# Attention maxima four heads at a time, in seven PSUM banks shared with the scores

## The chip, the cores and the metric

The kernel runs on one core of one Trainium2 chip. A core has TensorE (matmuls; PE in the profile, with its weight loads shown apart as PEld), VectorE (DVE), ScalarE (ACT), GpSimd (POOL) and SyncE (SP), which issues the transfers here. Matmul results go to PSUM, which this kernel uses as eight banks of 128 partitions by 512 float32 values; ScalarE and VectorE read them there. The metric is the device time of one execution in microseconds (us); lower is better.

## The reference

Two attentions over the same 2048 tokens (448 features, 16 heads of 28) are mixed by a gate per token:

```python
g = sigmoid((x * gate_w).sum(-1, keepdims=True))
# A: linear attention, feature maps phi = [softmax(q w_phi), softmax(-q w_phi)]
num = einsum("bhqf,bhfd->bhqd", phi_q, kv);  den = phi_q . z + 1e-6;  a = (num / den) @ wo_A
# B: softmax attention
scores = einsum("bhqd,bhkd->bhqk", q, k) * Dh ** -0.5
p = softmax(scores, axis=-1)
b = einsum("bhqk,bhkd->bhqd", p, v) @ wo_B
out = g * a + (1 - g) * b
```

The change touches only B. Its softmax subtracts, for each query and head, the largest score over all 2048 keys; these are the maxima of this document.

## The kernel before, in words

The front stage (to about 340 us) projects q, k and v, does attention A and computes the maxima of the first few batches. A batch `gq` is one group of four heads with one block of 512 queries; there are 16 batches. Then comes the attention stage of B: 256 steps `s`, sixteen to a batch, one for each block of 128 keys.

The order of the work is written out by hand on TensorE, VectorE, ScalarE and GpSimd: each engine runs its instructions in the order of the program, and a semaphore holds an instruction whose input or target isn't ready. Weight loads stand in TensorE's own order, so a load that waits holds everything behind it. A step issues, in this order:

- `scores(s, 0)` and `scores(s, 1)` (matmuls L831, exponentials L833): four matmuls, keys by queries, one per head, 128x512 each. The negated maxima are a row of the operands, so that the scores come out already shifted. Two heads fill a pair of banks, and one exponential on ScalarE reads both (128x1024).
- `values(s - 1)` (L934): the four heads' exponentials of the step before, times v, added up over sixteen steps in one bank, `pv`.
- `finish` after the sixteenth: VectorE and ScalarE copy `pv` out (L373); the normalization follows over the next ten steps, with a small reciprocal on VectorE, two products on GpSimd and a cast on ScalarE.
- `mx_visit()` (matmuls L306, reduction L314): a visit to the maxima of a later batch. Three scores of 128 queries by 512 keys go to a tile of three banks (four heads lie at four groups of 32 rows, so that the matmuls of different heads go side by side), and one reduction on VectorE takes the three largest values (128x1536 to 128x3). There are 720 such scores in this stage. After the last of a batch, `mx_reduce` appends three small VectorE instructions (L232, L236, L238), which run behind the next visit's reduction.

In the last group of heads, twelve steps also project an output tile (`project`, L108 and L948), followed by a second visit.

PSUM's eight banks: two pairs for scores (`ps2`), three for maxima (`psm`), one for `pv`. When all maxima are done, `spare_open` turns the three into a third pair and a bank for projections, and `tail_open` into three banks for the last output tiles.

Of the kernel before, what the change touches and what calls it, by code (L numbers as in the profile page):

```python
# [8 lines left out]
F32 = mybir.dt.float32  # L9
F32R = mybir.dt.float32r  # L10
U32 = mybir.dt.uint32
AF = mybir.ActivationFunctionType
ALU = mybir.AluOpType
AX = mybir.AxisListType
PSUM = bass.MemoryType.PSUM
DRAM = bass.MemoryType.DRAM

P = 128
S = 2048
D = 448  # L20
H = 16
DH = 28
GW = 112
NG = 4
NT = S // P
NQ = S // 512
SCALE = DH ** -0.5
# [12 lines left out]
def gated_mix_kernel(ctx, tc, xT, wqkB, wvB, wvA, wkAT, wqAT, phi, woA, woB,  # L40
# [7 lines left out]
    nc = tc.nc  # L48
# [35 lines left out]
    sel_s = const.tile([P, 4], F32, name="sel_s")  # L84
# [70 lines left out]
    mxs = {"u": 0, "f": 0, "fin": []}  # L155
# [3 lines left out]
    part = mxp.tile([P, NU * 4], F32, name="part", bufs=1)  # L159
# [24 lines left out]
    def mx_query(gq):  # L184
        g, qb = divmod(gq, NQ)
        mxs[("qc", gq)] = mx_rows(mx_tile("qc", f"qc{gq}", 3), range(4), q_d[g], range(4), qb * 512)
# [100 lines left out]
    def mx_visit():  # L287

        fins = mxs["fin"][:]
        mxs["fin"].clear()  # L290
        f = mxs["f"]
        todo = flats[f:f + 3]
        todo = [x for i, x in enumerate(todo) if x[4] == todo[0][4] + i]
        if not todo:
            for fn in fins:
                fn()
            return
        mxs["f"] = f + len(todo)
        pm = psm.tile([P, 3, 512], F32, tag="mx", name=f"pm{f}", bufs=1)
        for i, (gq, kb, qt, j, col) in enumerate(todo):  # L300
            g, qb = divmod(gq, NQ)
            if kb == 1 and qt in (0, QM) and j == 0 and gq + 1 < NG * NQ:
                if ("qc", gq + 1) not in mxs:
                    mx_query(gq + 1)
            js = slice(32 * j, 32 * j + DH)
            nc.tensor.matmul(pm[:, i, :], mxs[("qc", gq)][js, qt * P:(qt + 1) * P],  # L306
                             mxs[("kc", g, kb)][js, :], start=True, stop=True,
                             tile_position=(32 * j, 0))
            if j == 3 and qt == 3 and qb == NQ - 1 and g + 1 < NG:
                mx_load(g + 1, kb)  # L310
            if kb == 3 and qt == 3 and j == 3:
                mx_reduce(gq)
        n, col = len(todo), todo[0][4]
        nc.vector.tensor_reduce(part[:, col:col + n], pm[:, :n], AX.X, ALU.max)  # L314
        for fn in fins:
            fn()

# [501 lines left out]
    def scores(s, i):  # L819

        gq, kt = divmod(s, NT)
        g, qb = divmod(gq, NQ)
        if s:
            p = late_p.tile([P, 2, 512], F32, tag="p", name=f"p{s}_{i}", bufs=6)
            st = ps_p(f"st{s}_{i}", s == NS - 1)
        else:
            p = at.tile([P, 2, 512], F32, name=f"p{s}_{i}")
            st = ps_mx(f"st{s}_{i}", i)
        for jl in range(2):
            j = 2 * i + jl  # L830
            nc.tensor.matmul(st[:, jl, :], kst_of[(g, kt // 4)][:, j, (kt % 4) * P:(kt % 4 + 1) * P],  # L831
                             qst_of[gq][:, j, :], start=True, stop=True)
        nc.scalar.activation(p, st, AF.Exp, scale=SCALE)  # L833
        pts.setdefault(s, []).append(p)

    qst = [stack("qst0", False)]
    kst = [stack(f"kst{i}", True) for i in range(5)]
# [24 lines left out]
    ps_s_.close()  # L862
    fr_s.close()
    ps2 = ctx.enter_context(tc.tile_pool(name="ps2", bufs=1, space=PSUM, reuse_waits="tile"))
    psm_s, spare_s = ExitStack(), ExitStack()
    psm = psm_s.enter_context(tc.tile_pool(name="psm", bufs=1, space=PSUM, reuse_waits="tile"))

    spare = []
    turns = {"n": 0}

    def spare_open():
        psm_s.close()
        spare.append(spare_s.enter_context(
            tc.tile_pool(name="psx", bufs=1, space=PSUM, reuse_waits="tile")))

    def ps_p(nm, last=False):
        if spare and spare[0] is not None and not last:
            turns["n"] += 1
            if turns["n"] % 3 == 0:
                return spare[0].tile([P, 2, 512], F32, tag="p", name=nm, bufs=1)  # L880
        return ps2.tile([P, 2, 512], F32, tag="p", name=nm, bufs=2)

    late_p = ctx.enter_context(tc.tile_pool(name="late", bufs=1, reuse_waits="tile"))
    woB_s = late_p.tile([P, 2, 4, D], F32R, name="woB_s")
# [42 lines left out]
    def values(s):  # L927
        gq, kt = divmod(s, NT)
        g, qb = divmod(gq, NQ)
        if kt == 0:  # L930
            pv_of[gq] = ps2.tile([P, 512], F32, tag="pv", name=f"pv{gq}", bufs=1)
        pv, pt = pv_of[gq], pts.pop(s)
        for j in range(4):
            nc.tensor.matmul(pv[32 * j:32 * j + 32, :], vb[kt // 8][:, kt % 8, 4 * g + j, :],  # L934
                             pt[j // 2][:, j % 2, :],
                             start=kt == 0, stop=kt == NT - 1, tile_position=(0, 32 * j),
                             skip_group_check=True)

    def project(qb, oT, tl):

        t = qb * 4 + tl
        acc = acc_of[qb][:, tl, :]
        if spare:
            po = spare[0].tile([P, 512], F32, tag="po", name=f"pob{t}", bufs=1)
        else:
            po = ps_p(f"pob{t}")[:, 0, :]
        run(po[:, :D], first_passes(qb, tl) + out_passes(oT, tl * P, woB_s, NG - 1))
        nc.vector.scalar_tensor_tensor(acc, po[:, :D], gate1[:, t:t + 1], acc,  # L948
                                       op0=ALU.mult, op1=ALU.add)
        nc.sync.dma_start(out[0, t * P:(t + 1) * P, :], acc)  # L950
# [7 lines left out]
    tail = {"todo": []}  # L958

    def tail_open():  # L960
        spare_s.close()
        spare[0] = None
        pst = ctx.enter_context(tc.tile_pool(name="pst", bufs=1, space=PSUM, reuse_waits="tile"))
        tail["po"] = [pst.tile([P, 512], F32, name=f"poL{i}")[:, :D] for i in range(3)]
        for tl in range(4):
            tail["todo"] += [(tl, i == 0, x) for i, x in enumerate(first_passes(NQ - 1, tl))]

    def tail_fill(n):
        for _ in range(min(n, len(tail["todo"]))):
            tl, first, (l, r) = tail["todo"].pop(0)  # L970
            if tl == len(tail["po"]):
                tail["po"].append(ps_p("poL3")[:, 0, :D])
            nc.tensor.matmul(tail["po"][tl], l, r, start=first, stop=False,
                             skip_group_check=True)

# [34 lines left out]
    def finish_last(gq):  # L1010

        oU = late_p.tile([P, 512], F32, tag="oU", name="oUlast", bufs=2)
        nc.vector.tensor_copy(oU, pv_of[gq])
        tail_fill(4)
        pd = ps_p("pd")
        for tl in range(4):
            nc.tensor.matmul(pd[:, 0, 4 * tl:4 * tl + 4], oU[:, tl * P:(tl + 1) * P], sel_s,
                             start=True, stop=True)
        rc = late_p.tile([P, 16], F32, tag="den", name="rc", bufs=2)
        nc.vector.reciprocal(rc, pd[:, 0, :16])  # L1020
        oT = late_p.tile([P, 2, 512], F32R, tag="oT", name="oTlast", bufs=2)
        rw = late_p.tile([P, 16, 32], F32, tag="rs", name="rw", bufs=2)
        nc.vector.tensor_copy(rw, rc.unsqueeze(2).to_broadcast([P, 16, 32]))
        tail_fill(4)
        pr = pd[:, 1, :]
        for tl in range(4):
            nc.tensor.matmul(pr[:, tl * P:(tl + 1) * P],
                             rw[:, 4 * tl:4 * tl + 4, :].rearrange("p j d -> p (j d)"), ident,
                             start=True, stop=True)
        tail_fill(12)  # L1030
        for c in (0, 256):
            nc.vector.tensor_mul(oU[:, c:c + 256], oU[:, c:c + 256], pr[:, c:c + 256])
            nc.scalar.copy(oT[:, 0, c:c + 256], oU[:, c:c + 256])
        for c in (0, 256):
            nc.vector.tensor_sub(oT[:, 1, c:c + 256], oU[:, c:c + 256], f32(oT[:, 0, c:c + 256]))
        for tl in range(4):
            while tail["todo"] and tail["todo"][0][0] <= tl:
                tail_fill(1)
            po, t = tail["po"][tl], (NQ - 1) * 4 + tl
            acc = acc_of[NQ - 1][:, tl, :]  # L1040
            for i, (l, r) in enumerate(out_passes(oT, tl * P, woB_s, NG - 1)):
                nc.tensor.matmul(po, l, r, start=False, stop=i == 2, skip_group_check=True)
            nc.vector.scalar_tensor_tensor(acc, po, gate1[:, t:t + 1], acc,
                                           op0=ALU.mult, op1=ALU.add)
            nc.sync.dma_start(out[0, t * P:(t + 1) * P, :], acc)
# [9 lines left out]
    for s in range(NS + 16):  # L1055
# [29 lines left out]
            mx_fin()  # L1085
        if s in mids:
            mids.pop(s)()
            mx_visit()
        if mxs["f"] == len(flats) and not spare:
            spare_open()  # L1090
        if NG * NQ - 1 in nm_of and NG * NQ - 1 in qst_of:
# [71 lines left out]
```

## Time and profile before

| what | value |
|---|---|
| median of three runs | 1054.67 us (1054.39 to 1055.61) |
| the profiled execution | 1055.21 us |
| its span, first to last instruction | 1053.2 us |
| granted TensorE clock | 0.999 |
| busy: TensorE, ScalarE, VectorE, GpSimd | 99%, 69%, 67%, 22% of the span |
| exponentials (ScalarE, L833) | 512 of 1.02 us |
| reductions of maxima (VectorE, L314) | 241 |

A group's row gives line, engine, operation, names of tiles (out<-in), shapes and count, then busy time in us, the mean duration in ns, and the idle time of the engine just before with what ended it. A row in order of time gives start and length in us. The span is what the instructions cover; the time of an execution has about 2 us more around it. Matmuls are pipelined and their ends are modelled, so starts are the better measure on TensorE.

### The profile page before, as it was taken

The page shows a single profiled execution, that of the slowest core. Times are in us where ns is not written, and L with a number is a line of the kernel's source. Part 1 is how long each engine was busy: PE and PEld are TensorE (multiplying, and loading weights), DVE is VectorE, ACT ScalarE, POOL GpSimd, SP SyncE. Part 2 cuts the span into 40 slices and gives each one's busy share as a digit, 9 for nine tenths or more (in the row PEclk, how much of TensorE's full clock was granted, in tenths as well). Part 3 has the DMA queues.
Part 4 walks back from the last instruction along what each step waited for, and adds up shares of the span by engine and source line. Part 5 has one row for each costly group of instructions (what it writes and reads, how often), then busy time and mean ns, then how long its engine had stood idle before and what let it go on. Part 6 is the DMA issues. An engine that isn't in the chain of part 4 may idle for free.

```text
span 1053.2 us, 16588 instructions
## 1 busy us (share of the span) xinstructions
PE 1042.9 (99%) x6344; PEld 568.8 (54%) x6344; DVE 705.6 (67%) x872; ACT 726.7 (69%) x878; POOL 227.3 (22%) x189
## 2 busy tenths in 40 slices
PE   8999999999999999999999999999999999999998
PEld 7777777778777634334433433443343343454545
DVE  5476776897856567767776777677677777777302
ACT  5355555577855777887777777777777777747572
POOL 1234454678635500120000000000000000000000
PEclk9999999999999999999999999999999999999999
DMA  8873110122233832233522324422233344132311
GB/s 292 292 234 101 42 38 30 41 66 88 86 111 93 186 64 53 62 77 78 121 63 68 80 54 145 116 65 71 64 69 78 83 108 104 46 112 65 96 63 53
DMA packets 64183, 99.03 MB, mean 94 GB/s; under 512 B 18008, under 2 KB 24776, under 8 KB 64104
## 3 DMA queue, kind: packets, MB, share of 16 engines
q1 hardware_dynamic: 64104, 97.97, 34.0%
q8 instruction: 50, 0.82, 0.4%
q14 instruction: 29, 0.24, 0.1%
HBM read 69.77 MB, written 27.78 MB: 93 GB/s over the span
## 4 chain that ended last, share of the span: by engine, by line
PE 93%; DVE 5%; ACT 1%; POOL 1%; DMA 0%; issue 0%; DVEq 0%; ACTq 0%; POOLq 0%
PE st L831 27%; PE pv L934 24%; PE pm L306 10%; PE pqk L108 5%; PE poa L108 4%; PE pk L126 4%; PE pva L126 3%; PE pob L108 3%; PE pmb L267 3%; PE pvb L126 2%; PE pvb L108 2%; PE pq L108 1%; PE pn L507 1%; PE pft L495 1%; PE pqk L609 1%; DVE rl L272 1%
## 5 line engine op out<-in xcount | busy, mean ns | idle before, releaser
L833 ACT ACTIVATE p<-st 128x1024 f32<-128x1024 f32 x512 | 496.7, 1022 | 165.0 <-PE st L831 163.5
L314 DVE TENSOR_REDUCE part<-pm 128x3 f32<-128x1536 f32 (+1 forms) x241 | 421.9, 1751 | 168.5 <-PE pm L306 168.3
L831 PE MATMUL st<-qst,kst 128*128 128x512 f32 x1024 | 306.6, 421 | 0.0
L934 PE MATMUL pv<-p,vb 128*32 128x512 f32 x2048 | 272.7, 605 | 0.0
L831 PEld LDWEIGHTS st<-qst,kst 128*128 128x128 f32 x1024 | 172.5, 188 | 92.5 <-issue 67.4
L306 PEld LDWEIGHTS pm<-kc,qc 28*128 28x128 f32 x720 | 45.2, 181 | 199.4 <-DVE part L314 175.7
L272 DVE CUSTOM_DVE_ANT_0 rl<-pmb,rl 128x512 f32<-128x512 f32 x152 | 98.2, 684 | 54.8 <-ACT rl L270 54.7
L394 POOL TENSOR_TENSOR oUb<-oUb,rsb 128x512 f32<-128x512 f32 x15 | 19.2, 1282 | 518.4 <-DMA rsb<-rdb 313.7
L306 PE MATMUL pm<-kc,qc 28*128 28x512 f32 x720 | 121.2, 495 | 0.4 <-DVE part L314 0.4
L270 ACT ACTIVATE rl<-pmd 128x1024 f32<-128x1024 f32 x76 | 78.1, 1028 | 38.6 <-PE pmd L267 30.1
L934 PEld LDWEIGHTS pv<-p,vb 128*32 128x32 f32 x2048 | 40.3, 108 | 93.6 <-issue 92.8
L108 PE MATMUL pqk<-XH,wB 128*128 128x512 f32 x192 | 59.6, 397 | 1.7 <-DVE ev L547 1.7
L108 PE MATMUL poa<-woA_s,oTa 128*128 128x448 f32 x192 | 43.4, 375 | 0.0
L546 ACT CAST ev<-pqk 128x512 fp32r<-128x512 f32 x28 | 15.9, 588 | 36.5 <-PE pqk L108 32.1
L108 PEld LDWEIGHTS pqk<-XH,wB 128*128 128x128 f32 x192 | 35.3, 188 | 10.5 <-DVE ev L547 2.1
L126 PE MATMUL pk<-wkA_s,XH 128*128 128x448 f32 x128 | 39.4, 381 | 0.0
L267 PE MATMUL pmd<-kp,qp 28*128 28x512 f32 x152 | 37.9, 494 | 1.0 <-DVE part L272 1.0
L108 PEld LDWEIGHTS poa<-woA_s,oTa 128*128 128x128 f32 x192 | 34.9, 188 | 6.3 <-issue 3.3
L267 PE MATMUL pmb<-kp,qp 28*128 28x512 f32 x152 | 38.0, 495 | 0.0
L126 PE MATMUL pva<-wvA_s,XH 128*128 128x450 f32 x128 | 37.8, 371 | 0.0
L108 PE MATMUL pq<-wqA_s,XH 128*128 128x448 f32 x128 | 37.3, 374 | 0.2 <-ACT oUa L370 0.2
L948 DVE SCALAR_TENSOR_TENSOR acc<-pob,gate,acc 128x448 f32<-128x448 f32 x12 | 8.2, 684 | 41.6 <-PE pob L108 41.6
(150 smaller groups left out, 1072.7 us busy)
## 6 DMA issues: line engine op xcount, KB each, us to landing
qkd<-ev SPq DMA_DIRECT2D x28, 512.0 KB
qst<-qkd SPq DMA_DIRECT2D x64, 224.0 KB
kst<-qkd SPq DMA_DIRECT2D x64, 224.0 KB
od<-oTb SPq DMA_DIRECT2D x48, 112.0 KB
rsa<-rda SPq DMA_DIRECT2D x8, 512.0 KB
rsb<-rdb SPq DMA_DIRECT2D x15, 256.0 KB
gad<-ga SPq DMA_DIRECT2D x16, 224.0 KB
acc<-gad SPq DMA_DIRECT2D x4, 896.0 KB
```

The source lines that it names most:

```text
L108: nc.tensor.matmul(dst, l, r, start=i == 0, stop=i == len(todo) - 1)
L126: nc.tensor.matmul(dst[:, :n], l, r, start=i == 0, stop=i == len(todo) - 1, skip_group_check=True)
L267: nc.tensor.matmul((pb if j < 2 else pd)[:, j % 2, :], qc[js, qt * P:(qt + 1) * P], kc[js, :], start=True, stop=True, tile_position=(32 * ...
L270: nc.scalar.activation(rl, pd, AF.Relu)
L272: nc.vector.tensor_tensor_reduce(rl[:, i, :], pb[:, i, :], rl[:, i, :], 1.0, LOWEST, ALU.add, ALU.max, part[:, col + i:col + i + 1])
L306: nc.tensor.matmul(pm[:, i, :], mxs[("qc", gq)][js, qt * P:(qt + 1) * P], mxs[("kc", g, kb)][js, :], start=True, stop=True, tile_position= ...
L314: nc.vector.tensor_reduce(part[:, col:col + n], pm[:, :n], AX.X, ALU.max)
L394: (nc.gpsimd if n == 1 else nc.vector).tensor_mul(oU, oU, rs)
L546: nc.scalar.copy(e[:, 0, :], pq)
L831: nc.tensor.matmul(st[:, jl, :], kst_of[(g, kt // 4)][:, j, (kt % 4) * P:(kt % 4 + 1) * P], qst_of[gq][:, j, :], start=True, stop=True)
L833: nc.scalar.activation(p, st, AF.Exp, scale=SCALE)
L934: nc.tensor.matmul(pv[32 * j:32 * j + 32, :], vb[kt // 8][:, kt % 8, 4 * g + j, :], pt[j // 2][:, j % 2, :], start=kt == 0, stop=kt == NT ...
```

## The change

One pool of seven banks (`free`, tags g0 to g6) serves scores and maxima. Each score takes one bank off the front of the list, gets an exponential of its own (128x512; 1024 of them and no longer 512) and its own tile of results. A visit takes four banks for the four heads of one query block against one key block, four matmuls and four reductions of one bank each, so that there are 180 visits. The visit's first bank goes back on the list at once; the other three wait in `held` and are returned, interleaved with the step's four score banks, behind the second `scores` of the next step. Returning a bank to the list is a matter of the program's text: whoever takes it waits, on the chip, for the instruction that last reads it. The second visit behind a projection is gone. After the last visit the held banks go back and one bank is set aside for projections; the end of the kernel takes its banks from the same list.

```diff
-        todo = flats[f:f + 3]
-        todo = [x for i, x in enumerate(todo) if x[4] == todo[0][4] + i]
...
+        todo = flats[f:f + 4]
         mxs["f"] = f + len(todo)
-        pm = psm.tile([P, 3, 512], F32, tag="mx", name=f"pm{f}", bufs=1)
...
+            pm = mx_banks(f)
+            for j in range(4):
+                js = slice(32 * j, 32 * j + DH)
+                nc.tensor.matmul(pm[j], mxs[("qc", gq)][js, qt * P:(qt + 1) * P],
+                                 mxs[("kc", g, kb)][js, :], start=True, stop=True,
+                                 tile_position=(32 * j, 0))
+            for j in range(4):
+                nc.vector.tensor_reduce(part[:, col + j:col + j + 1], pm[j], AX.X, ALU.max)
...
-        n, col = len(todo), todo[0][4]
-        nc.vector.tensor_reduce(part[:, col:col + n], pm[:, :n], AX.X, ALU.max)
         for fn in fins:
             fn()
@@ scores(s, i) @@
-        if s:
-            p = late_p.tile([P, 2, 512], F32, tag="p", name=f"p{s}_{i}", bufs=6)
-            st = ps_p(f"st{s}_{i}", s == NS - 1)
...
-        nc.scalar.activation(p, st, AF.Exp, scale=SCALE)
-        pts.setdefault(s, []).append(p)
+        sts = []
+        for j in (2 * i, 2 * i + 1):
+            used.append(free.pop(0))
+            sts.append(bank(used[-1], f"st{s}_{j}"))
+            score(j, sts[-1])
+        for st in sts:
+            p = late_p.tile([P, 512], F32, tag="p", name=f"p{s}_{len(pts.get(s, []))}", bufs=12)
+            nc.scalar.activation(p, st, AF.Exp, scale=SCALE)
+            pts.setdefault(s, []).append(p)
+        if i == 1:
+            a, m = used[:], held[:]
+            free.extend([a[0], m[0], a[1], m[1], a[2], a[3], m[2]] if m else a)
+            used.clear()
+            held.clear()
@@ pools @@
+    free, used, held = list(range(7)), [], []
+    def bank(i, nm):
+        return ps2.tile([P, 512], F32, tag=f"g{i}", name=nm, bufs=1)
+
+    def mx_banks(f):
+        b = [free.pop(0) for _ in range(4)]
+        free.append(b[0])
+        held.extend(b[1:])
+        return [bank(i, f"pm{f}_{j}") for j, i in enumerate(b)]
 
     def spare_open():
+        free.extend(held)
+        held.clear()
+        spare.append(free.pop())
@@ project @@
-        if spare:
-            po = spare[0].tile([P, 512], F32, tag="po", name=f"pob{t}", bufs=1)
-        else:
-            po = ps_p(f"pob{t}")[:, 0, :]
+        po = bank(spare[0], f"pob{t}")
@@ the loop over steps @@
         if s in mids:
             mids.pop(s)()
-            mx_visit()
```

More of the change, by code (lines that the diff above doesn't have):

```diff
@@ L291, in mx_visit @@
         f = mxs["f"]
-        todo = flats[f:f + 3]
-        todo = [x for i, x in enumerate(todo) if x[4] == todo[0][4] + i]
[L294 to L297, printed above, removed]
+        todo = flats[f:f + 4]
         mxs["f"] = f + len(todo)
-        pm = psm.tile([P, 3, 512], F32, tag="mx", name=f"pm{f}", bufs=1)
-        for i, (gq, kb, qt, j, col) in enumerate(todo):
+        if todo:
+            gq, kb, qt, _, col = todo[0]
             g, qb = divmod(gq, NQ)
[L302 to L309, printed above, removed]
+            if kb == 1 and qt in (0, QM) and gq + 1 < NG * NQ and ("qc", gq + 1) not in mxs:
+                mx_query(gq + 1)
+            pm = mx_banks(f)
[6 more added lines that the diff above has]
+                nc.vector.tensor_reduce(part[:, col + j:col + j + 1], pm[j], AX.X, ALU.max)
+            if qt == 3 and qb == NQ - 1 and g + 1 < NG:
                 mx_load(g + 1, kb)
-            if kb == 3 and qt == 3 and j == 3:
+            if qt == 3 and kb == 3:
                 mx_reduce(gq)
-        n, col = len(todo), todo[0][4]
-        nc.vector.tensor_reduce(part[:, col:col + n], pm[:, :n], AX.X, ALU.max)
         for fn in fins:
@@ L822, in scores, with score @@
         g, qb = divmod(gq, NQ)
-        if s:
-            p = late_p.tile([P, 2, 512], F32, tag="p", name=f"p{s}_{i}", bufs=6)
-            st = ps_p(f"st{s}_{i}", s == NS - 1)
-        else:
+        def score(j, st):
+            nc.tensor.matmul(st, kst_of[(g, kt // 4)][:, j, (kt % 4) * P:(kt % 4 + 1) * P],
+                             qst_of[gq][:, j, :], start=True, stop=True)
+        if s == 0:
             p = at.tile([P, 2, 512], F32, name=f"p{s}_{i}")
             st = ps_mx(f"st{s}_{i}", i)
[L829 to L833, printed above, removed]
-        pts.setdefault(s, []).append(p)
+            for jl in range(2):
+                score(2 * i + jl, st[:, jl, :])
+            nc.scalar.activation(p, st, AF.Exp, scale=SCALE)
+            pts.setdefault(s, []).extend([p[:, 0, :], p[:, 1, :]])
+            return
+        sts = []
[5 more added lines that the diff above has]
+            p = late_p.tile([P, 512], F32, tag="p", name=f"p{s}_{len(pts.get(s, []))}", bufs=12)
+            nc.scalar.activation(p, st, AF.Exp, scale=SCALE)
+            pts.setdefault(s, []).append(p)
[4 more added lines that the diff above has]
+            held.clear()
     qst = [stack("qst0", False)]
@@ L864, in gated_mix_kernel @@
     ps2 = ctx.enter_context(tc.tile_pool(name="ps2", bufs=1, space=PSUM, reuse_waits="tile"))
-    psm_s, spare_s = ExitStack(), ExitStack()
-    psm = psm_s.enter_context(tc.tile_pool(name="psm", bufs=1, space=PSUM, reuse_waits="tile"))
+    free, used, held = list(range(7)), [], []
     spare = []
-    turns = {"n": 0}
-    def spare_open():
[L872 to L881, printed above, removed]
+    def bank(i, nm):
[5 more added lines that the diff above has]
+        return [bank(i, f"pm{f}_{j}") for j, i in enumerate(b)]
+    def spare_open():
+        free.extend(held)
+        held.clear()
+        spare.append(free.pop())
     late_p = ctx.enter_context(tc.tile_pool(name="late", bufs=1, reuse_waits="tile"))
@@ L934, in values @@
             nc.tensor.matmul(pv[32 * j:32 * j + 32, :], vb[kt // 8][:, kt % 8, 4 * g + j, :],
-                             pt[j // 2][:, j % 2, :],
+                             pt[j],
                              start=kt == 0, stop=kt == NT - 1, tile_position=(0, 32 * j),
@@ L942, in project @@
         acc = acc_of[qb][:, tl, :]
-        if spare:
-            po = spare[0].tile([P, 512], F32, tag="po", name=f"pob{t}", bufs=1)
-        else:
-            po = ps_p(f"pob{t}")[:, 0, :]
+        po = bank(spare[0], f"pob{t}")
         run(po[:, :D], first_passes(qb, tl) + out_passes(oT, tl * P, woB_s, NG - 1))
@@ L960, in tail_open @@
     def tail_open():
[L961 to L964, printed above, removed]
+        tail["po"] = [bank(i, f"poL{n}")[:, :D]
+                      for n, i in enumerate([spare[0], free.pop(0), free.pop(0)])]
         for tl in range(4):
@@ L971, in tail_fill @@
             if tl == len(tail["po"]):
-                tail["po"].append(ps_p("poL3")[:, 0, :D])
+                tail["po"].append(bank(free.pop(0), "poL3")[:, :D])
             nc.tensor.matmul(tail["po"][tl], l, r, start=first, stop=False,
@@ L1014, in finish_last @@
         tail_fill(4)
-        pd = ps_p("pd")
+        pd = bank(free.pop(0), "pd")
         for tl in range(4):
-            nc.tensor.matmul(pd[:, 0, 4 * tl:4 * tl + 4], oU[:, tl * P:(tl + 1) * P], sel_s,
+            nc.tensor.matmul(pd[:, 4 * tl:4 * tl + 4], oU[:, tl * P:(tl + 1) * P], sel_s,
                              start=True, stop=True)
         rc = late_p.tile([P, 16], F32, tag="den", name="rc", bufs=2)
-        nc.vector.reciprocal(rc, pd[:, 0, :16])
+        nc.vector.reciprocal(rc, pd[:, :16])
         oT = late_p.tile([P, 2, 512], F32R, tag="oT", name="oTlast", bufs=2)
@@ L1024, in finish_last @@
         tail_fill(4)
-        pr = pd[:, 1, :]
+        pr = bank(free.pop(0), "pr")
         for tl in range(4):
```

## The prediction

> **What bounds the kernel now.** I read the page first (busy shares, chain, groups), then the order of time inside one step of the attention stage, then the few rows that price a short instruction or a late one.
>
> ```profile
> span 1053.2 us, 16588 instructions
> ...
> PE 1042.9 (99%) x6344; PEld 568.8 (54%) x6344; DVE 705.6 (67%) x872; ACT 726.7 (69%) x878; POOL 227.3 (22%) x189
> ...
> PE 93%; DVE 5%; ACT 1%; POOL 1%; DMA 0%; issue 0%; DVEq 0%; ACTq 0%; POOLq 0%
> PE st L831 27%; PE pv L934 24%; PE pm L306 10%; PE pqk L108 5%; PE poa L108 4%; PE pk L126 4%; PE pva L126 3%; PE pob L108 3%; PE pmb L267 3%; PE pvb L126 2%; PE pvb L108 2%; PE pq L108 1%; PE pn L507 1%; PE pft L495 1%; PE pqk L609 1%; DVE rl L272 1%
> ...
> L314 DVE TENSOR_REDUCE part<-pm 128x3 f32<-128x1536 f32 (+1 forms) x241 | 421.9, 1751 | 168.5 <-PE pm L306 168.3
> ```
>
> TensorE is the path: the chain that ended last is 93% TensorE, and 27 + 24 + 10% of it are scores (L831), values (L934) and maxima (L306). VectorE and ScalarE work two thirds of the span. The reduction of the maxima runs 241 times. In order of time, one step (start and length in us):
>
> ```profile
> 602.35 1.20 PE L831 MATMUL st<-qst,kst 128*128 128x512 f32 x4
> 603.48 1.06 PE L934 MATMUL pv<-p,vb 128*32 128x512 f32 x8
> 604.48 0.50 PE L306 MATMUL pm<-kc,qc 28*128 28x512 f32 x3
> 604.91 1.21 PE L831 MATMUL st<-qst,kst 128*128 128x512 f32 x4
> 605.03 1.76 DVE L314 TENSOR_REDUCE part<-pm 128x3 f32<-128x1536 f32 x1 [0.81 <-PE pm L306]
> 605.73 0.40 PE L831 MATMUL st<-qst,kst 128*128 128x512 f32 x1
> 605.75 1.94 ACT L833 ACTIVATE p<-st 128x1024 f32<-128x1024 f32 x2 [0.63 <-PE st L831]
> ```
>
> A step lasts 2.56 us (602.35 to 604.91). TensorE passes from scores to values after 1.13 (602.35 to 603.48), from values to maxima after 1.00, from maxima to the next scores after 0.43 (604.48 to 604.91). VectorE waits 0.81 per step and ScalarE 0.63: neither holds TensorE up. The steps after the last maxima:
>
> ```profile
> 998.03 1.19 PE L831 MATMUL st<-qst,kst 128*128 128x512 f32 x4
> 999.15 1.06 PE L934 MATMUL pv<-p,vb 128*32 128x512 f32 x8
> 1000.15 1.19 PE L831 MATMUL st<-qst,kst 128*128 128x512 f32 x4
> ```
>
> 2.12 us. A visit of maxima costs TensorE 0.435 us, between the 0.43 above and this difference of 0.44.
>
> **The change, part by part.** (a) *Fewer visits.* 720 heads of maxima in threes took 241 visits (the cut between two batches costs one); in fours they take 180. A visit's price does not grow with the fourth head if four row tiles go side by side as three do. The front stage has four such matmuls in a unit:
>
> ```profile
> 271.79 0.50 PE L267 MATMUL pmd<-kp,qp 28*128 28x512 f32 x2
> 272.22 0.84 PEld L495 LDWEIGHTS pft<-ident,featq 128*112 128x112 f32 x8 [0.25 <-issue]
> ```
>
> Next work again 0.43 after their start. So 61 x 0.435 = 26.5 us less on TensorE. The visits then end at step 180 and not near step 236.
>
> (b) *Projections.* Eight of the twelve mid-step projections had a second visit behind them and shared the pairs of banks:
>
> ```profile
> 917.48 0.76 PEld L831 LDWEIGHTS st<-qst,kst 128*128 128x128 f32 x4 [0.24 <-issue]
> 922.90 0.76 PEld L831 LDWEIGHTS st<-qst,kst 128*128 128x128 f32 x4 [0.25 <-issue]
> ```
>
> and, behind the last visit,
>
> ```profile
> 1019.25 0.86 PEld L831 LDWEIGHTS st<-qst,kst 128*128 128x128 f32 x4
> 1023.62 0.86 PEld L831 LDWEIGHTS st<-qst,kst 128*128 128x128 f32 x4
> ```
>
> 5.42 less two visits (0.87) is 4.55, against 4.37 without visits: 8 x 0.15 = 1.2 us less.
>
> (c) *The hand-out of banks.* Before, maxima had three banks of their own and the two pairs of scores had two each. Followed by hand, the new list settles at once: scores 1 and 2 of a step take the banks of scores 3 and 4 of the step before (free when their exponentials end), score 3 takes that of head 4 of the maxima two visits back, and **score 4 takes that of head 1 of the visit just ahead of it**. Heads 1 and 3 take the banks of this step's scores 1 and 2, heads 2 and 4 those of heads 2 and 3 of the last visit. The built program shows these waits: ScalarE, ScalarE, VectorE, VectorE for scores 1 to 4. The order on TensorE is unchanged (scores, values, maxima), so score 4 now stands, with all values and maxima queued behind it, until the first reduction of the last visit has ended. Nothing in the old order had that wait. The rows for its price are a visit of a single head that the trace happens to have, with the last score of the same step,
>
> ```profile
> 376.79 0.50 PE L306 MATMUL pm<-kc,qc 28*128 28x512 f32 x1
> 377.33 0.69 DVE L314 TENSOR_REDUCE part<-pm 128x1 f32<-128x512 f32 x1 [0.72 <-PE pm L306]
> ...
> 378.02 0.40 PE L831 MATMUL st<-qst,kst 128*128 128x512 f32 x1
> ```
>
> a score's weight load that waited for VectorE,
>
> ```profile
> 928.00 0.68 DVE L948 SCALAR_TENSOR_TENSOR acc<-pob,gate,acc 128x448 f32<-128x448 f32 x1 [0.62 <-PE pob L108]
> ...
> 928.73 0.19 PEld L831 LDWEIGHTS st<-qst,kst 128*128 128x128 f32 x1
> ```
>
> and the second and third score of the step shown above:
>
> ```profile
> 605.25 0.40 PE L831 MATMUL st<-qst,kst 128*128 128x512 f32 x1
> 605.49 0.63 PE L831 MATMUL st<-qst,kst 128*128 128x512 f32 x2
> ```
>
> The reduction started 0.54 after the matmul and took 0.69; the load started 0.05 after VectorE's end (928.68 to 928.73). So score 4's load starts 0.54 + 0.69 + 0.05 = 1.28 after the maxima. A load that runs ahead is hidden; the first score of a step, whose load doesn't, holds the array 0.34 (604.91 to 605.25) where the next holds it 0.24, so a late load costs 0.10 more, and score 4 runs from 1.38. Today it starts 1.23 (376.79 to 378.02) or 1.25 (604.48 to 605.73) after the maxima. The delay is 0.14 and the step becomes 2.70. It follows 179 visits: 179 x 0.14 = 25.1 us. Bounds: 0.05 if only the matmul and not its load waited (1.28 against 1.24), 9 us; 0.23 if nothing of the load's 0.19 is hidden (1.28 + 0.19 - 1.24), 41 us. I take 0.14, from the first score, whose load is late in the same way.
>
> (d) *Four short reductions for a long one.* The long one, 1.76 for three banks, and the single one give 0.535 for each further bank and 0.155 fixed. How much of that is covered when they follow each other, and what else VectorE does in this stage, stands here:
>
> ```profile
> 599.92 1.76 DVE L314 TENSOR_REDUCE part<-pm 128x3 f32<-128x1536 f32 x1 [0.74 <-PE pm L306]
> 601.60 0.25 DVE L232 TENSOR_REDUCE red<-part 128x16 f32<-128x64 f32 x1
> 601.88 0.17 DVE L236 TENSOR_SCALAR neg<-red 128x16 fp32r<-128x16 f32 x1
> 602.10 0.21 DVE L238 STREAM_TRANSPOSE nm<-neg 128x32 f32<-128x32 f32 x1
> ...
> 607.26 0.56 DVE L373 COPY oUb<-pv 128x384 f32<-128x384 f32 x1 [0.47 <-PE pv L934]
> ```
>
> The next instruction starts 1.68 after a 1.76: 0.08 is covered, so one single takes 0.61 and four 2.44, inside a step of 2.70. The slack, though, falls from 0.8 to 0.26, and what sat in it comes out. Once per sixteen steps the chain of three small instructions (601.60 to about 602.24, 0.63) makes the next first reduction, and so score 4, 0.37 late. Once per sixteen, the copy of the values (0.56, 0.48 of it not covered) is done 0.22 after the point where that reduction was due: VectorE is free 0.54 + 2.44 - 2.70 = 0.28 after the maxima, the copy is through at 0.76, due was 0.54. The small reciprocal just fits. Eleven of each fall ahead of step 180: 11 x 0.59 = 6.5 us.
>
> The Trainium skill has a rule on this, in Perfetto Trace Analysis, section Optimizing Scalar/DVE Operations: each VectorE operation pays about 125 ns for data access on PSUM, and grouping into larger operations helps where the engine is saturated. By that fixed cost a single would take an estimated 0.66, the slack would be 0.06, and the extras would come to about 13 us in place of 6.5, for a total near 1066; the pair 1.76 and 1.68 above speaks for 0.075 fixed and not 0.125.
>
> (e) *Single exponentials.* A pair of 1024-wide ones takes 1.94, the second ending 1.02 after its start, so 0.92 each. The nearest row for 512 columns out of a PSUM bank is
>
> ```profile
> 271.55 1.06 ACT L498 COPY fT<-pft 112x512 f32<-112x512 f32 x2
> ```
>
> with 0.59 for one, so 0.47 between starts; half of 0.92 is the other end, and I take 0.49 (0.92 less the 0.43 between the durations 1.02 and 0.59); without any overlap it would be 0.59. Four cost 1.96 per step, against 1.84, under both 2.70 and 2.12. The first starts earlier and the last ends no later, so values don't wait. A cast of that width once per sixteen steps delays the bank of score 2 by up to 0.4, most of it inside score 4's wait: 1 us in all.
>
> (f) *End of the kernel*: banks by name in place of pairs, same matmuls, all released before they are asked for: 0, within 0.3.
>
> Sum against the profiled execution's 1055.21 (its span 1053.2 and 2.0 around it; 0.5 over the median of the runs): -26.5 - 1.2 + 25.1 + 6.5 + 1 = +4.9, or 1060.1, and 1059.5 in terms of the median.
>
> **The rivals.** *Faster: the hand-off is cheap.* If the wait holds the matmul alone, the delay is 0.05 per step, 9 us, and the sum is 1054.67 - 27.7 + 9 + 7.4 = 1043. For it: a load at 928.73 was 0.07 late and the next matmul not at all. Against it: the loads carry the waits in this trace. It decides as soon as the delay is under 0.11 per step (20 us). With no delay and no extras it would end at 1027, which needs a first reduction 0.3 us earlier than any row.
>
> *No change*: a delay of 0.11 to 0.13 and extras of 5 us give 1053 to 1056; nothing in the rows excludes it.
>
> *VectorE becomes the bound.* If singles, each with its own wait, don't overlap at all, four take 2.77, and with 0.08 of other work per step the pace is 2.85: 179 x 0.29 = 52 and no extras beside, 1054.67 - 27.7 + 52 + 1 = 1080. Against it: back-to-back rows overlap throughout.
>
> *ScalarE becomes the bound behind step 180.* Without overlap four exponentials are 4 x 0.59 = 2.36, over 2.12: 75 x 0.3 = 22 us on top, 1082. Against it the 0.92 and 0.47 above.
>
> **How the numbers follow.** Forecast 0.58 (its own range 1055 to 1068, from delays of 0.12 to 0.18); cheap hand-off 0.16; no change 0.12; VectorE 0.09; ScalarE 0.05. From 1043 to 1076 leaves out half of the cheap case and most of the last two, some 0.2. A measurement here can tell about 0.2%, 2.1 us, from no change. Faster by more: 0.17; within: 0.14; slower: 0.69.
>
> **What would show it.** Reductions of one bank at 0.61 apart, 180 visits. Steps of 2.70 up to step 180, with the last score's weight load waiting for VectorE, then 2.12 at once. A wait of score 4 that isn't there, or steps of 2.56, would make me wrong towards 1030; steps of 2.85 with VectorE full towards 1080. Two longer steps in each sixteen, by 0.37 and 0.22, show the extras.

## The result, and the profile after

The changed kernel takes 1061.27 us in the median of four runs (1060.55 to 1062.47) against 1054.53 for the kernel before: a ratio of 1.0062, with a 95% interval of 1.005 to 1.0075. It is slower by 0.6%, where 1059.5 (1043 to 1076) was forecast.

The page of the kernel after, busy times, chain and three groups:

```profile
span 1060.4 us, 17608 instructions
...
PE 1046.2 (99%) x6344; PEld 559.5 (53%) x6344; DVE 727.2 (69%) x1351; ACT 756.3 (71%) x1388; POOL 227.8 (21%) x189
...
PE 87%; DVE 7%; DMA 2%; ACT 1%; SPq 1%; issue 1%; POOL 0%; ACTq 0%; DVEq 0%; POOLq 0%
...
L306 DVE TENSOR_REDUCE part<-pm 128x1 f32<-128x512 f32 x720 | 446.7, 683 | 36.1 <-PE pm L302 35.4
L821 PE MATMUL st<-qst,kst 128*128 128x512 f32 x1024 | 334.7, 439 | 5.0 <-DMA qst<-nm 1.9
...
L302 PE MATMUL pm<-kc,qc 28*128 28x512 f32 x720 | 90.9, 495 | 0.0
```

The visits' matmuls fell from 121.2 to 90.9 us busy, as they should. TensorE still reads 99% busy, although it now waits in most steps: ends of matmuls are modelled, and the wait turns up as busy time, in a group of the scores that grew from 306.6 to 334.7 us. What shows it is the view of waits of the weight loads (PEld), where this row is new (us in total, times, longest):

```profile
PEld st L821 <- DVE part L306: 61.7, 180, 0.8
```

and the order of time in one step:

```profile
602.82 0.51 PE L302 MATMUL pm<-kc,qc 28*128 28x512 f32 x4
...
603.25 0.53 PEld L821 LDWEIGHTS st<-qst,kst 128*128 128x128 f32 x3 [0.24 <-ACT p L839]
603.25 1.34 PE L821 MATMUL st<-qst,kst 128*128 128x512 f32 x4
603.35 2.48 DVE L306 TENSOR_REDUCE part<-pm 128x1 f32<-128x512 f32 x4 [0.21 <-PE pm L302]
603.79 2.07 ACT L839 ACTIVATE p<-st 128x512 f32<-128x512 f32 x4 [0.63 <-PE st L821]
604.09 0.19 PEld L821 LDWEIGHTS st<-qst,kst 128*128 128x128 f32 x1 [0.31 <-DVE part L306]
604.52 0.16 PEld L947 LDWEIGHTS pv<-p,vb 128*32 128x32 f32 x8 [0.25 <-issue]
604.52 1.07 PE L947 MATMUL pv<-p,vb 128*32 128x512 f32 x8
605.52 0.19 PEld L302 LDWEIGHTS pm<-kc,qc 28*128 28x128 f32 x4 [0.84 <-ACT p L839]
605.52 0.50 PE L302 MATMUL pm<-kc,qc 28*128 28x512 f32 x4
```

Three weight loads of the scores follow each other, the fourth comes 1.27 us after the maxima, released by the reduction. The step lasts 2.70 (602.82 to 605.52). Without visits, from step 181 on, it is 2.12 again:

```profile
867.19 1.19 PE L821 MATMUL st<-qst,kst 128*128 128x512 f32 x4
868.32 1.06 PE L947 MATMUL pv<-p,vb 128*32 128x512 f32 x8
869.31 0.96 PE L821 MATMUL st<-qst,kst 128*128 128x512 f32 x3
```

By the starts of each step's first score, steps 1 to 180 took 460.4 us before and 492.1 now (+31.7), steps 181 to 254 took 212.2 and 187.7 (-24.5); ahead of step 1 and behind step 254 nothing changed by more than 0.2. That is the span's +7.2.

Two further kinds of longer steps occur. Twice in sixteen VectorE's small work delays the first reduction (VectorE's rows, then the copy with the maxima ahead of it):

```profile
769.76 2.48 DVE L306 TENSOR_REDUCE part<-pm 128x1 f32<-128x512 f32 x4 [0.23 <-PE pm L302]
772.16 0.25 DVE L232 TENSOR_REDUCE red<-part 128x16 f32<-128x64 f32 x1
...
772.65 0.21 DVE L238 STREAM_TRANSPOSE nm<-neg 128x32 f32<-128x32 f32 x1
772.79 2.44 DVE L306 TENSOR_REDUCE part<-pm 128x1 f32<-128x512 f32 x4
```

```profile
799.24 0.19 PEld L302 LDWEIGHTS pm<-kc,qc 28*128 28x128 f32 x4 [0.84 <-ACT p L839]
...
799.47 0.55 DVE L369 COPY oUb<-pv 128x384 f32<-128x384 f32 x1
799.93 0.68 DVE L306 TENSOR_REDUCE part<-pm 128x1 f32<-128x512 f32 x1
```

And at two changes of the group of heads (steps 63 and 191) TensorE waits for transfers, which it did not before; the second of them:

```profile
879.73 1.17 PE L821 MATMUL st<-qst,kst 128*128 128x512 f32 x4 [1.86 <-DMA qst<-nm]
```

### The profile page after: what moved, and what is told of

The parts are those of the page before. It is cut to its first block, busy times and chain, and to the rows that moved or that the text cites. A ratio compares the mean times of both kernels' runs of the same rounds, so it can differ in the third digit from the quotient of the medians.

```text
span 1060.4 us, 17608 instructions
## 1 busy us (share of the span) xinstructions
PE 1046.2 (99%) x6344; PEld 559.5 (53%) x6344; DVE 727.2 (69%) x1351; ACT 756.3 (71%) x1388; POOL 227.8 (21%) x189
## 4 chain that ended last, share of the span: by engine, by line
PE 87%; DVE 7%; DMA 2%; ACT 1%; SPq 1%; issue 1%; POOL 0%; ACTq 0%; DVEq 0%; POOLq 0%
PE st L821 26%; PE pv L947 21%; PE pm L302 7%; PE pqk L108 6%; PE pk L126 4%; PE poa L108 3%; PE pva L126 3%; DVE part L306 3%; PE pob L108 3%; PE pmb L267 3%; PE pq L108 2%; PE pvb L126 2%; PE pvb L108 1%; PE pn L503 1%; PE pqk L605 1%; DMA kst<-qkd 1%
## 5 line engine op out<-in xcount | busy, mean ns | idle before, releaser
L839 ACT ACTIVATE p<-st 128x512 f32<-128x512 f32 x1020 | 526.0, 607 | 137.9 <-PE st L821 134.7
L306 DVE TENSOR_REDUCE part<-pm 128x1 f32<-128x512 f32 x720 | 446.7, 683 | 36.1 <-PE pm L302 35.4
L821 PE MATMUL st<-qst,kst 128*128 128x512 f32 x1024 | 334.7, 439 | 5.0 <-DMA qst<-nm 1.9
L302 PEld LDWEIGHTS pm<-kc,qc 28*128 28x128 f32 x720 | 34.4, 181 | 150.9 <-ACT p L839 150.1
L302 PE MATMUL pm<-kc,qc 28*128 28x512 f32 x720 | 90.9, 495 | 0.0
L369 DVE COPY oUb<-pv 128x384 f32<-128x384 f32 x15 | 8.3, 551 | 68.9 <-PE pv L947 68.9
```

The lines of the kernel that those rows point to most:

```text
L302: nc.tensor.matmul(pm[j], mxs[("qc", gq)][js, qt * P:(qt + 1) * P], mxs[("kc", g, kb)][js, :], start=True, stop=True, tile_position=(32 * ...
L306: nc.vector.tensor_reduce(part[:, col + j:col + j + 1], pm[j], AX.X, ALU.max)
L821: nc.tensor.matmul(st, kst_of[(g, kt // 4)][:, j, (kt % 4) * P:(kt % 4 + 1) * P], qst_of[gq][:, j, :], start=True, stop=True)
```

## The experiments

The theory to test: the last score of a step waits for the first reduction of the visit ahead of it, because the shared list gives it that bank, and this eats what the 61 visits save. Rivals: many short instructions hold TensorE up whatever the banks; a fourth head makes a visit dearer; VectorE's sum of work sets the pace.

**Short instructions, own banks.**

```diff
-        todo = flats[f:f + 4]
+        todo = flats[f:f + 3]
...
-            pm = mx_banks(f)
...
+        pm = [bank(4 + i, f"pm{f}_{i}") for i in range(len(todo))]
...
-    free, used, held = list(range(7)), [], []
+    free, used, held = list(range(4)), [], []
```

> Single exponentials and single reductions as in the changed kernel, but three heads to a visit and banks of their own: four for scores, three for maxima, one second visit behind each projection as before. Theory (the last score of a step waits for the first reduction of the visit ahead of it): no such wait here, steps back at 2.56 us, 241 visits, total 1053 to 1057, level with the kernel before. Rival (the many short instructions with their semaphores hold TensorE up, whatever the banks): steps stay near 2.70 and, with 61 visits more, the total goes to 1080 or over.

1056.13 us against 1054.57, a ratio of 1.0016 (1.0007 to 1.0025), in its profile:

```profile
600.05 0.76 PEld L821 LDWEIGHTS st<-qst,kst 128*128 128x128 f32 x4 [0.24 <-issue]
...
602.60 0.77 PEld L821 LDWEIGHTS st<-qst,kst 128*128 128x128 f32 x4 [0.24 <-issue]
```

All four loads run in a row and the step is 2.55 (2.56 in the median). A thousand exponentials and 720 reductions in place of 512 and 241 cost no time in the steps. Of the 0.16% (1.6 us) that remain, about half is one step of 3.42 at a change of the group of heads, which waits for a transfer, and another of 2.98, against one of 3.02 before. The first rival falls.

**No first reduction.**

```diff
+    nc.gpsimd.memset(part, 0.0)
...
-            for j in range(4):
+            for j in range(1, 4):
                 nc.vector.tensor_reduce(part[:, col + j:col + j + 1], pm[j], AX.X, ALU.max)
```

> The changed kernel with the reduction of each visit's first head left out (its maxima stand at 0, so the softmax is shifted by less than it should be for a quarter of the heads). All four matmuls of a visit stay. Theory: the last score's bank has no reader to wait for, steps of 2.56 with visits, the small VectorE work fits into the slack again, total 1061.3 - 26 - 5 = 1030. Rival (the fourth head costs TensorE by itself): steps stay near 2.70, total 1061.

1032.48 us, a ratio of 0.9794 (0.9779 to 0.9809).

```profile
599.63 0.51 PE L303 MATMUL pm<-kc,qc 28*128 28x512 f32 x4
600.07 0.76 PEld L822 LDWEIGHTS st<-qst,kst 128*128 128x128 f32 x4 [0.24 <-issue]
...
602.18 0.51 PE L303 MATMUL pm<-kc,qc 28*128 28x512 f32 x4
```

Four heads in the visit and still 2.55 to 2.58 a step: the fourth head is free on TensorE (0.44 from maxima to scores), and the second rival falls. The total is 2.5 us over the expectation. Two steps at changes of the group took 4.38 and 3.85, so the transfers wait here too; but these waits come to 3.5 us, and the 1061.3 from which the expectation was worked out has 4.5 us of them, so they don't explain the 2.5, which stay open.

**The first two reductions exchanged.**

```diff
-            for j in range(4):
+            for j in (1, 0, 2, 3):
                 nc.vector.tensor_reduce(part[:, col + j:col + j + 1], pm[j], AX.X, ALU.max)
```

> The changed kernel with the first two reductions of every visit in exchanged order, nothing else. Theory: the last score waits for one more reduction, 0.60 us per visit, steps of 3.30 up to step 180, total 1061.3 + 179 x 0.60 = 1168, a little less where VectorE's small work disappears in the longer step. Rival (VectorE's sum of work or the number of instructions sets the pace): no change, 1061.

1163.15 us in one run, for the same instructions in the same number.

```profile
601.57 0.51 PE L302 MATMUL pm<-kc,qc 28*128 28x512 f32 x4
...
602.01 0.98 PE L821 MATMUL st<-qst,kst 128*128 128x512 f32 x3
602.11 2.49 DVE L306 TENSOR_REDUCE part<-pm 128x1 f32<-128x512 f32 x4 [0.83 <-PE pm L302]
...
603.45 0.19 PEld L821 LDWEIGHTS st<-qst,kst 128*128 128x128 f32 x1 [0.91 <-DVE part L306]
```

The fourth load now comes 1.88 after the maxima and not 1.27, one reduction later, and the step is 3.31 (3.30 expected). VectorE idles 0.83 per step, so its sum of work cannot be what sets the pace: the third rival falls as well. The total is 5 us under 1168. By the starts of the steps about half of that lies ahead of step 181, where the three small instructions are hidden again (those steps take 3.30; the ones with the copy still up to 3.44), and half behind it, where most of the waits for transfers are gone.

**The small work out of the way.** The three small instructions each stand behind a visit of their own, and ScalarE copies all of `pv`:

```diff
-        fins = mxs["fin"][:]
-        mxs["fin"].clear()
+        fins = mxs["fin"][:1]
+        del mxs["fin"][:1]
...
-            if n == 2:
+            if i < n:
                 nc.scalar.copy(oU[:, i, :], pn[i])
-            else:
-                c = slice(384 * i, 384 + 128 * i)
-                (nc.scalar.copy if i else nc.vector.tensor_copy)(oU[:, 0, c], pn[0][:, c])
```

> The changed kernel with the three small VectorE instructions behind a batch's maxima put behind three visits, one each, and the copy of the values all on ScalarE. Theory: the two longer steps in each sixteen (0.29 and 0.15 over 2.70) become ordinary, 11 x 0.44 = 4.8 us less, total 1056.4. Rival (those longer steps come from elsewhere, transfers or ScalarE): within 1 us of 1061.3.

1056.44 us, 1.0015 of before (1.0007 to 1.0024). The steps of 3.00 and 2.85 are gone (steps 1 to 180: 487.7 us against 492.1), all ordinary ones are 2.70. Two single steps of 3.56 and 3.24 are new in this profile. In the first:

```profile
597.81 1.28 POOL L393 TENSOR_TENSOR oUb<-oUb,rsb 128x512 f32<-128x512 f32 x1 [35.78 <-DMA rsb<-rdb]
597.85 1.26 DVE L240 TENSOR_SCALAR neg<-red 128x16 fp32r<-128x16 f32 x1
...
599.03 2.47 DVE L312 TENSOR_REDUCE part<-pm 128x1 f32<-128x512 f32 x4
...
599.76 0.19 PEld L824 LDWEIGHTS st<-qst,kst 128*128 128x128 f32 x1 [1.17 <-DVE part L312]
```

The small instruction that makes `neg`, 0.17 us elsewhere, took 1.26 (0.94 in the second of these steps) and ended 0.03 after a product on GpSimd that had started ahead of it; the first reduction came late by that much, and the fourth load behind it. In the attention stages of these profiles `neg` took longer than 0.2 us nine times, and each time it ended 0.03 after such a product. That the product holds it up is read from these rows; no run moved the one away from the other.

**Earlier loads.**

```diff
-            if kt == 12 and gq + 1 < NG * NQ:
+            if kt == 7 and gq + 1 < NG * NQ:
                 load_q(gq + 1)
-            if kt == (12 if gq + 1 < 14 else 14) and gq + 1 < NG * NQ - 1:
+            if kt == 7 and gq + 1 < NG * NQ - 1:
```

> The changed kernel with the query block and the row of maxima of the next batch asked for in the eighth step of a batch and not in the thirteenth, nothing else. Theory (the steps of 3.76, 4.05 and 3.05 us at the changes of the group of heads wait for transfers that are queued late behind the stores of the finished batch): these steps become ordinary, 3 to 4.5 us less, 1057 to 1058.5. Rival (those waits belong to the keys' blocks, which stay where they are): no change, 1061.

1057.36 us, 1.0026 of before (1.0016 to 1.0036). No step of this profile waits for a transfer: step 63, 191, 192 and 193, 3.76, 4.05, 2.69 and 3.05 in the changed kernel, are now 2.69, 2.12, 2.12 and 2.17. For step 63 the view of waits of the changed kernel names a block of keys. This edit did not move those requests, but four of them stood behind the moved ones in SyncE's queue. Which transfer step 63 waited for was not separated.

**Three scores behind a visit.** What follows from the theory is a way round the wait: three banks are always free behind a visit, and only the fourth score needs the reduced one. On top of the last two edits (the rows of maxima of the last batches are still asked for late), a step with a visit issues three scores, and every fourth step issues four more in place of a visit.

```diff
-                scores(s, 0)
-                scores(s, 1)
+                next_scores(3 if deep else 4 * s + 4 - stream["n"])
...
-        if s:
+        if s < NS and deep and s % 4 == 1:
+            next_scores(4)
+        elif s:
             mx_visit()
```

> Built on the kernel with the spread small work and the earlier loads: a step with a visit issues three scores and no longer four, and every fourth step issues four further scores in place of a visit (up to step 208; the last 24 visits stand in steps of four scores as before); banks are picked by the earliest estimated release. Theory: with three scores behind a visit none needs the first reduced bank, and the 0.145 us of waiting per visit go; four steps cost 2.23 + 2 x 2.33 + 2.94 = 9.8 us by the intervals on TensorE, 10.0 with ScalarE's backlog behind seven scores in a row, against 3 x 2.70 + 2.12 = 10.2: 1056.4 - 3.5 - 10 = 1043, between 1035 and 1052. Rival (VectorE's 2.4 us per visit or the backlog on ScalarE set the pace as soon as the steps get shorter): 1053 or more.

1060.67 us, 1.0058 of before (1.0044 to 1.0071): a miss. Four steps took 10.28 and not 10.0. The wait for the reduction behind each visit is gone, but behind the seven scores in a row another has taken its place, on ScalarE, which had all seven banks to empty (the weight loads of a step behind a visit, then those of the step behind the seven):

```profile
601.55 0.51 PE L308 MATMUL pm<-kc,qc 28*128 28x512 f32 x4
601.98 0.53 PEld L842 LDWEIGHTS st<-qst,kst 128*128 128x128 f32 x3 [0.25 <-issue]
...
607.58 0.19 PEld L842 LDWEIGHTS st<-qst,kst 128*128 128x128 f32 x1 [0.25 <-ACT p L851]
608.07 0.19 PEld L842 LDWEIGHTS st<-qst,kst 128*128 128x128 f32 x1 [0.30 <-ACT p L851]
```

With every third step and three scores more instead:

> As the last run, but every third step (up to step 156) issues three further scores in place of a visit, so that six and not seven follow each other; the other 76 visits up to step 232 stand in steps of four scores. Theory (what the last run lost, 0.44 us in four steps, is ScalarE's backlog behind seven scores that fill all seven banks): with six, one bank is left for the next step and the backlog is gone; three steps cost 2.22 + 2.33 + 2.70 = 7.25 against 2 x 2.70 + 2.12 = 7.52, 52 x 0.27 = 14 us less than spread work and earlier loads alone (1061.3 - 4.9 - 3.9 = 1052.5): 1038, between 1033 and 1046. Rival (the change of order itself costs TensorE as much as it saves): 1052 or more.

1050.21 us, 0.9955 of before (0.9937 to 0.9973): the fastest of the kernels that take all maxima, under the kernel before by 0.45%, but 12 us short of the 1038 expected. Three steps took 7.45 and not 7.25. The weight loads behind six scores, in order of time:

```profile
545.39 0.19 PEld L308 LDWEIGHTS pm<-kc,qc 28*128 28x128 f32 x4 [0.84 <-issue]
546.03 0.19 PEld L842 LDWEIGHTS st<-qst,kst 128*128 128x128 f32 x1 [0.45 <-ACT p L851]
546.52 0.19 PEld L842 LDWEIGHTS st<-qst,kst 128*128 128x128 f32 x1 [0.30 <-ACT p L851]
547.01 0.19 PEld L842 LDWEIGHTS st<-qst,kst 128*128 128x128 f32 x1 [0.30 <-ACT p L851]
```

They come 0.49 apart, ScalarE's pace. The last run asked whether it was the choice of banks again:

```diff
         b = sorted(avail, key=lambda b: rel[b])[:4]
+        n = max(4, sum(rel[i] <= clk["pe"] + 150 for i in b))
+        b = b[n - 4:n]
```

> As the last run (1050.2), but a visit takes those four released banks that came free last and leaves the bank released first to the score behind it. In the last run the visit behind six scores took the one bank that was left, and the three scores behind it waited for ScalarE (starts 546.03, 546.52, 547.01), 0.20 us in three steps. Theory (which bank goes to whom sets this wait too): three steps from 7.45 to 7.25 or 7.30, 52 x 0.15 to 0.20 = 8 to 10 us less, 1040 to 1042. Rival (ScalarE's rate behind six scores sets it, whatever the bank): 1050.

1050.25 us, 0.9959 of before (0.9945 to 0.9973), three steps again 7.45. The wait only moved to the visit's last head:

```profile
544.42 0.19 PEld L308 LDWEIGHTS pm<-kc,qc 28*128 28x128 f32 x3 [0.84 <-issue]
545.06 0.18 PEld L308 LDWEIGHTS pm<-kc,qc 28*128 28x128 f32 x1 [0.45 <-ACT p L851]
```

So here the rival held: behind a run of six scores it is ScalarE's rate, whoever gets the bank. That is 52 x 0.2 = 10 of the 12 us by which the run with six scores fell short. In its profile the other 2 lie in a few longer groups of three steps (three of 7.96, one of 7.76, one of 7.81); what lengthens them was not followed up.

## Why the prediction was right

Point by point, in its own steps:

(a) *Visits* and (b) *projections*: with the transfers' waits taken away (the run with earlier loads) steps 181 to 254 took 184.3 us against 212.2 before, 27.9 less; forecast were 26.5 + 1.2 = 27.7. The four matmuls of a visit hold TensorE 0.43 to 0.44, like three. Of the 27.9, 0.46 is a single step of 3.02 in the kernel before (step 201), in which `neg` took 1.13 us beside a product on GpSimd; without it 27.4 are left. In (b) two readings were off and cancelled by luck: the visits before end at step 235, so six of the projections and not eight had a second visit behind them, and the rows shown give 4.55 - 4.37 = 0.18 for each and not 0.15, which makes 1.1 where 1.2 was put down.

(c) *The hand-out of banks*: the wait is where it was put, and of its size. The reduction started 0.53 after the maxima (forecast 0.54) and took 0.69, the load came at 1.27 (1.28), values 0.43 behind it (0.42 by the forecast's sum), the step took 2.70 (2.70). The excess over the 2.556 median before is 0.145 to 0.15 per step, 26 us over 179 steps (25.1). That the load and not only the matmul waits, on which the faster rival hung, is shown by the row at 604.09. Leaving the reduction out and putting it off by one moved the time by -28.8 and +102 us, so the cause is shown and not only argued.

(d) *Four short reductions*: they start 0.60 apart (2.48 for four, the last taking 0.68), as the covered 0.08 had it; the 0.61 of the forecast was 0.01 too long. The slack was therefore 0.30, and the two kinds of longer steps cost 0.29 and 0.15 and not 0.37 and 0.22: 4.9 us in place of 6.5. The run with the small work spread gave 4.8 back, net of 1.4 us that its two new long steps took, so this match is closer than the terms behind it. By the fixed cost of about 125 ns on PSUM from the Trainium skill's Perfetto Trace Analysis, section Optimizing Scalar/DVE Operations, four would have taken an estimated 2.64 and these steps some 13 us; the measured fixed part that is not covered is 0.06 to 0.07 us (0.60 less the 0.535 for a bank), half the page's figure, and the measurement decides.

(e) *Single exponentials*: 0.48 to 0.49 apart (2.07 for four, one taking 0.61), forecast 0.49; no time lost to them, as the run with banks of their own shows. The 1 us put down for the casts did not appear. (The rival on ScalarE was priced at 0.3 us a step, 22 us; its own figures, 2.36 and 2.12, give 0.24 and 18 us, or some 1078.)

What the forecast did not have is the transfers: 1.06 + 1.93 + 0.57 + 0.93 us in four steps, some 4 us by the run with earlier loads; none of it is in the kernel before. Shorter steps behind step 180 leave less time between the request for the next batch's data and its use, but that is not the whole of it: with the first two reductions exchanged these steps are as short, and step 191 takes only 0.33 us more than the others. The first of the waits stands at step 63, where steps were longer than before, and the run with banks of its own has one there too, with steps as long as before; why, was not settled. So the near match of 1059.5 and 1061.3 is in part luck, two errors of opposite sign: 2.6 us too much for small work and casts, and 4 us missing.

## What to carry to other kernels

When buffers are shared, follow the list by hand until it repeats, and ask of each user in the order of the bounding engine which instruction it now waits for: a saving on that engine (0.435 us for each of 61 visits) was matched by a 0.145 us wait repeated 179 times. A wait is priced by adding start, duration, release and the exposed part of a weight load from rows of the old trace, and a single odd instruction in it (one reduction of one bank among 241) can be the best row there is. A cure that bunches the same work moves the wait to the next engine in line, so it needs the same walk through the buffers once more.

## What the runs showed that was not expected

A busy share of 99% on TensorE stood both with and without a wait of 0.145 us in every step; starts and the weight loads' idle time showed it, the busy share did not. Doubling the number of exponentials cost ScalarE only 0.04 us per pair (two in 0.48 + 0.48 against one in 0.92) and cost the kernel nothing. Requests moved five steps earlier in a queue were worth 4 us, nearly as much as the small VectorE work. And a VectorE instruction of 0.17 us took up to 1.26 where a GpSimd product ran beside it: one such meeting cost TensorE up to 0.9 us (a step of 3.56 and not 2.70).
